# Seven edits to the order of work in a fused attention and mixture-of-depths kernel

## The chip, the cores and the metric

The kernel runs on one core of a Trainium2 chip. The metric is the device time of one execution in microseconds (us), of which several runs are taken. A core has five engines that run side by side and wait for one another by semaphores: TensorE (PE, matrix products and transposes; its weight loads are listed as PEld), VectorE (DVE), ScalarE (ACT), GpSimd (POOL) and SyncE (SP), which here only issues transfers (DMAs). Each engine takes its instructions in the order in which the program emits them.

## The reference, cut to what matters

```python
# attention, per batch (8) and head (12), sequence 448, head size 64
q_n = q / sqrt(mean(q*q) + 1e-6) * g_q          # k_n likewise, with g_k
attn = softmax(q_n @ k_n.T / sqrt(64))
x = concatenate heads of (attn @ v)             # [8, 448, 768]
# mixture of depths, per batch
scores = x @ w_gate                             # [448]
top = the 128 tokens with the highest scores
h = maximum(x[top] @ w1, 0)                     # w1 [768, 1024]
out = x;  out[top] = x[top] + sigmoid(scores[top])[:, None] * (h @ w2)   # w2 [1024, 768]
```

All is float32.

## The kernel before, in words

**Groups and units.** The attention is cut into 24 groups (`q`, or `n`, from 0 to 23), three for each batch, of four heads each. A group has seven units of 64 keys. For a unit, `scores` (L337) multiplies keys by queries into two PSUM banks of the pool `ps_sc` (four banks), and two exponentials on ACT (L346) write a probability tile `p` (seven buffers, two heads side by side). The key's norm is applied as the scale of the exponential. `values` (L361) multiplies the values by `p`. `add_probs` adds the probability tiles of a group on DVE (L377), so that `sum_keys` (L404) can get the denominators by small products on PE with `pick_pair`. `by_array(n)` says for how many of a group's last units that addition is left out: these tiles are kept in `lasts` and given to PE as further terms of the same sum. After that, `invert_sums` transposes and inverts the denominators (`rden`, L420) and `to_tokens` transposes the result to tokens and scales it (L435, L437) into the batch's tile `x`.

**Norms.** Queries and keys come in twice, transposed for the products (`qT`, `kT`) and by tokens (`tok`). `squares` (L255, ACT) squares a `tok` tile into one of two buffers `sqs`, `sum_squares` (L264, DVE) sums it and POOL raises the sum to the power -1/2 (L265). For queries this goes out to DRAM (`rows_out`, L276), comes back spread over the partitions (`rows_in`, `bc`, L287), and `scale_q` (L296, DVE) multiplies `qT` by it before the group's scores. `prepare` (L773) sets the times of all this for a group.

**The mixture.** For each batch, `gate` (L463, DVE) takes the products of `x` and the gate's weights after every group, 256 columns at a time; `spread` sums the three parts. `ranks_of` transposes the gate's scores so that every token sees all (L488 on PE, L494 on ACT), `count` (L504, DVE) counts the higher ones, `annotate` writes gate and token number into two more columns of `x`, and `select` scatters the chosen rows to DRAM by four indirect DMAs from POOL (L531). `load_selected` (L549) reads them back by SP into `xe`, which has three buffers. `mixture(g)` then works on two batches at once, as a block product with seven products instead of eight in each of the two layers (a scheme of Strassen's kind): weights are kept as three blocks and four differences (numbers 0 to 3). In the first mixture the differences are made on DVE (`mix`, L244), stored to DRAM (`mixed`, L224) and later read back (`load_mixed`, L221) into a ring of three buffers; `used` asks for the next one when one is done. Products go to a PSUM bank `main`, or to a `side` bank that is taken from `ps_sc`. `share` copies or adds a product into the hidden layer (L658 on ACT, L660 on DVE), and the relu of a sum is L662 on ACT. `gated` (L578, DVE) applies the gate to the second layer's products, and `write` (L569) scatters the rows to the output from POOL.

**Order.** The schedule is written out by hand. The emission order is the order of each engine's queue. `at(slot, fn)` puts a call in a list under a unit's number, and `run(upto)` calls all that are due. Groups 0 to 7 have two places for that, after units 3 and 6. From group 8 on (`FIRST`) all seven units of a group come first (a stretch), and then three gaps: denominators of the group before, `run(u0 + 1)` and a piece of the mixture; `invert_sums`, the first `to_tokens`, `run(u0 + 3)` and a piece; the second `to_tokens`, `run(u0 + 6)` and in some groups a piece. `soon()` gives the present slot. After the last group the remaining pieces run one after another: this is the tail.

Of the kernel before, what the change touches and what calls it, by code (L numbers as in the profile page):

```python
# [68 lines left out]
def fast(  # L69
# [156 lines left out]
    def mix(l, i, part):  # L226

        if part == 0:
            if i == 3:
                in_ring(l, 3)  # L230
            elif i == 1:
                ring[l, 1] = ring[l, "B12"]
            elif i == 2:
                in_ring(l, 2)
            else:
                ring[l, 0] = ring[l, 2]
        a, b = {
            3: (blocks[l, (1, 1)], ring[l, "B12"]),
            1: (ring[l, "B12"], blocks[l, (0, 0)]),
            2: (blocks[l, (1, 1)], ring.get((l, 1))),  # L240
            0: (blocks[l, (1, 0)], ring.get((l, 2))),
        }[i]
        f = chunk(part)
        nc.vector.tensor_tensor(out=ring[l, i][:, f], in0=a[:, f], in1=b[:, f], op=OP.subtract)  # L244
# [145 lines left out]
    def by_array(n):  # L390

        return 2 if n < 2 * NG else 1 if n == n_groups - 1 else 0
# [62 lines left out]
    def gate(n):  # L455

        b, g = divmod(n, NG)
        if g == 0:
            gates[b] = moe_pool.tile([CP, NJ, NG], F32, name="gate_parts", bufs=2)
        cols = slice(GH * D * g, GH * D * (g + 1))  # L460
        for j in range(NJ):
            prod = moe_pool.tile([CP, S], F32, tag="wide", name="prod")
            nc.vector.scalar_tensor_tensor(  # L463
                out=prod[:, 0 : GH * D],
                in0=xs[b][:, j, cols],
                scalar=1.0,
                in1=wg[:, cols],
                op0=OP.mult,
                op1=OP.mult,
                accum_out=gates[b][:, j, g : g + 1],  # L470
            )
# [75 lines left out]
    def load_selected(b):  # L547
        xe = moe_pool.tile([128, DX], F32, name="xe", bufs=3)
        nc.sync.dma_start(out=xe[:CAP], in_=slots_dram.pop(b))  # L549
        xes[b] = xe  # L550
# [4 lines left out]
    def mixture(g):  # L555
# [41 lines left out]
        def used(l, i):  # L597

            if not to_load or g == 0 and (l == 1 or i == 2):
                return  # L600
            what = to_load.pop(0)
            s = soon()
            for part in range(2):
                at(s + 4 + 2 * part if s >= 0 else s, load_mixed, *what, part)
# [47 lines left out]
        def share(k, ps, begun):  # L652
            h = {1: h11, 2: h12, 3: h21, 4: h22}[k]
            ps = ps.rearrange(flat, t=128)[:, :, :n]
            missing[k] -= 1
            last_one = missing[k] == 0
            if not begun:
                nc.scalar.activation(out=h[:, :, :n], in_=ps, func=AF.Relu if last_one else AF.Copy)  # L658
                return
            nc.vector.tensor_tensor(out=h[:, :, :n], in0=h[:, :, :n], in1=ps, op=OP.add)  # L660
            if last_one:
                nc.scalar.activation(out=h[:, :, :n], in_=h[:, :, :n], func=AF.Relu)  # L662

        begun = set()
# [9 lines left out]
        for k in (1, 2, 3, 6, 5, 7, 4) if g == 0 else (1, 2, 6, 5, 7, 3, 4):  # L674
            in_main, what, a, targets = todo_products[k]
            ps = main if in_main else side()
            product(ps, weights(1, what), a(), k == 1 or not in_main)
            for t in targets:
                share(t, ps, t in begun)
                begun.add(t)  # L680
# [8 lines left out]
            if g == 0:  # L689
                if k == 5:  # L690
                    mix_all(1, 0)
                if k == 7:
                    for part in range(2):
                        load_block(2, (0, 1), part)
            yield
# [27 lines left out]
        for k in (1, 2, 6, 5, 7, 3, 4):  # L723
# [24 lines left out]
            if g == 0:  # L748
                if k == 1:
                    mix_all(2, 3)  # L750
                    mix_all(2, 1)
                if k == 2:
                    mix_all(2, 2)
                if k == 5:
# [18 lines left out]
    def prepare(n, slot):  # L773
        sq = {}
        for i in range(2):
            at(slot + 2 * i, lambda i=i: sq.setdefault(i, squares(n, i)))
            at(slot + 2 * i + 1, lambda i=i: sum_squares(n, i, sq.pop(i)))

        at(slot + (7 if n > 2 else 6), rows_out, n)
        at(slot + (10 if n > 5 else 9 if n > 2 else 8), rows_in, n)  # L780

    for n in range(1, n_groups):
# [4 lines left out]
        if n > 1:  # L787
# [3 lines left out]
            first = max(s0 - (20 if n > 5 else 17), 0)  # L791
            prepare(n, first)
            at(max(s0 - 6, first + 11), scale_q, n)
# [3 lines left out]
    for k, i in enumerate((3, 1, 2)):  # L797
        for part in range(2):
            at(NI * FIRST + 2 * k + part, mix, 1, i, part)
            at(NI * FIRST + 2 * k + part + 3, store_mixed, 1, i, part)  # L800
# [3 lines left out]
    def after_tokens(n):  # L804
        b, g = divmod(n, NG)
        s = soon()
        at(s + (2 if n == 1 else 0), gate, n)
# [3 lines left out]
        at(s + 4 if s >= 0 else s, store_x, b)  # L811
        at(s + 1 if s >= 0 else s, spread, b)

    def ranks_of(b):
# [6 lines left out]
        at(s + 7 if s >= 0 else s, load_selected, b)  # L821
# [28 lines left out]

    def run(upto):
# [13 lines left out]
    for q in range(n_groups):  # L865
# [4 lines left out]
        if q < FIRST:  # L870
            for place, us in enumerate(((0, 1, 2, 3), (4, 5, 6))):
                for i in us[::2]:
# [3 lines left out]
                    run_values(u0 + i - 1 if i < NI - 1 else u0 + i - 2, hold=i == us[2])  # L876
                slot[0] = u0 + us[0]
# [20 lines left out]
        for i in range(0, NI, 2):  # L898
# [3 lines left out]
            run_values(u0 + i - 1 if i < NI - 1 else u0 + i - 2)  # L902
        slot[0] = u0
# [3 lines left out]
        if g == 1 and b > 2:  # L907
# [3 lines left out]
        slot[0] = u0 + 2  # L911
        invert_sums(q - 1)
# [561 lines left out]
```

## Time and profile before

| | us |
|---|---|
| median of 3 runs (546.56 to 550.29) | 548.3 |
| the profiled execution | 549.26 |
| its span, first to last instruction | 547.5 |
| PE busy | 492.2 |
| DVE busy | 381.1 |
| ACT busy | 284.5 |
| POOL busy | 189.7 |

All times in the text are from the start of the span. In lists of groups, a line names the code line, the engine, the operation, what it writes and reads, how often, the busy time in all and the mean of one in ns. In lists of waits, a line says who waited for whom, the total, how often, and the longest. In the timeline a line has start, length, engine, code line, operation and tiles; `[5.79 <-DVE hT L660]` is the idle time of that engine before it and what ended it. Stages: start-up until 11.5, groups 0 to 7 until some 141, groups 8 to 23 with mixtures 0 to 2 until some 458, then the tail with the rest of mixture 2, the last batch's ranks and mixture 3.

### The profile page before, as it was taken

How to read it: one execution, taken by the hardware profiler on the slowest of the kernel's cores; microseconds unless marked ns; L12 is line 12 of the kernel's file. 1: busy time of each engine (PE TensorE's matmuls, PEld its weight loads, DVE VectorE, ACT ScalarE, POOL GpSimd, SP SyncE). 2: the span in 40 equal slices, each digit the busy share in tenths (PEclk: the TensorE clock that was granted, in tenths of full speed). 3: DMA queues.
4: the chain of work that ended last, by engine and by line, in shares of the span. 5: the costliest groups of instructions: out<-in, count | busy, mean ns of one | idle time of the engine just before them, and what ended most of it. 6: DMA issues, size and time to landing. Idle time of an engine off the chain costs nothing. (4 is left out here: it accounts for less than half of the span.)

```text
span 547.5 us, 11644 instructions
## 1 busy us (share of the span) xinstructions
PE 492.2 (90%) x4605; PEld 295.7 (54%) x4605; DVE 381.1 (70%) x718; ACT 284.5 (52%) x519; POOL 189.7 (35%) x104
## 2 busy tenths in 40 slices
PE   5979999989959889799979999999979999939990
PEld 4534444434726574364556785554455657628860
DVE  4653779799984767899878687887977784812240
ACT  4875788767626457365656647538565662002100
POOL 4682355744350307123452307321660030110002
PEclk9998999999979899999999999999999999978997
DMA  8877889799693473877778683979392351445711
GB/s 313 328 227 261 260 256 303 237 312 302 225 282 117 155 265 95 291 251 276 265 249 266 204 274 109 295 239 342 98 277 84 104 172 60 167 146 192 228 63 62
DMA packets 54449, 118.43 MB, mean 216 GB/s; under 512 B 12115, under 2 KB 26452, under 8 KB 54386
## 3 DMA queue, kind: packets, MB, share of 16 engines
q1 hardware_dynamic: 50978, 111.28, 63.1%
q0 software_dynamic: 3264, 6.31, 3.5%
q8 instruction: 38, 0.62, 0.5%
q14 instruction: 25, 0.20, 0.1%
q10 hardware_dynamic: 144, 0.00, 0.0%
HBM read 93.81 MB, written 31.64 MB: 229 GB/s over the span
## 5 line engine op out<-in xcount | busy, mean ns | idle before, releaser
L346 ACT ACTIVATE p<-sc,rinv 128x448 f32<-128x448 f32 x336 | 188.3, 640 | 92.7 <-issue 48.3
L265 POOL TENSOR_TENSOR rinv<-ss,neg_half 128x14 f32<-128x14 f32 (+1 forms) x49 | 134.2, 2742 | 196.4 <-DVE ss L264 146.6
L337 PE MATMUL sc<-qT,kT 64*64 64x448 f32 x1344 | 171.9, 553 | 14.5 <-DVE hT L660 5.8
L361 PE MATMUL av<-p,v 64*64 64x448 f32 x1344 | 165.5, 548 | 0.4 <-ACT xT L384 0.3
L377 DVE TENSOR_TENSOR sum<-sum,p 128x896 f32<-128x896 f32 x107 | 116.8, 1091 | 16.3 <-ACT p L346 11.0
L337 PEld LDWEIGHTS sc<-qT,kT 64*64 64x64 f32 x1344 | 61.8, 134 | 85.3 <-issue 43.7
L361 PEld LDWEIGHTS av<-p,v 64*64 64x64 f32 x1344 | 68.2, 136 | 65.9 <-issue 54.5
L531 POOL DMA_INDIRECT selected<-x,rank x32 | 39.7, 1240 | 68.6 <-DVE x L523 60.4
L264 DVE TENSOR_REDUCE ss<-sq 128x14 f32<-128x910 f32 (+1 forms) x49 | 52.3, 1072 | 0.7 <-ACT sq L255 0.7
L437 DVE TENSOR_TENSOR x<-x_ps,rden 112x512 f32<-112x512 f32 x48 | 32.8, 688 | 22.5 <-PE x_ps L435 20.6
L255 ACT ACTIVATE sq<-tok 128x896 f32<-128x896 f32 (+1 forms) x49 | 44.3, 936 | 7.3 <-DMA tok<-in_tok_dram 3.2
L463 DVE SCALAR_TENSOR_TENSOR prod<-x,wg 112x256 f32<-112x256 f32 x96 | 40.6, 423 | 2.6
L569 POOL DMA_INDIRECT out_dram<-xe,row x10 | 9.8, 984 | 85.8 <-DVE xe L578 37.9
L435 PE MATMUL x_ps<-ident,xT 128*112 128x128 f32 x192 | 29.1, 275 | 5.1 <-DVE rden L420 5.1
L578 DVE SCALAR_TENSOR_TENSOR xe<-moe_ps,xe 128x384 f32<-128x384 f32 (+2 forms) x17 | 10.0, 590 | 32.9 <-PE moe_ps L705 32.9
L662 ACT ACTIVATE hT<-hT 128x512 f32<-128x512 f32 x12 | 7.6, 630 | 46.5 <-DVE hT L660 46.5
L504 DVE SCALAR_TENSOR_TENSOR cmp<-score_rows,gate,earlier 112x448 f32<-112x448 f32 x32 | 21.8, 683 | 13.2 <-ACT score_rows L494 12.5
L384 ACT COPY xT<-av 128x448 f32<-128x448 f32 x48 | 23.4, 539 | 10.1 <-PE av L361 6.9
L377 DVE TENSOR_TENSOR sum<-p 128x896 f32<-128x896 f32 x24 | 26.1, 1086 | 2.1 <-ACT p L346 2.1
L435 PEld LDWEIGHTS x_ps<-ident,xT 128*112 128x112 f32 x192 | 21.6, 133 | 10.3 <-DVE rden L420 6.9
L296 DVE SCALAR_TENSOR_TENSOR qT<-qT,gg,bc 128x896 f32<-128x896 f32 x22 | 25.2, 1145 | 0.0
L643 PE MATMUL moe_ps<-xeT,ring 128*128 128x128 f32 x192 | 23.1, 277 | 1.8 <-DVE hT L660 1.8
(83 smaller groups left out, 459.1 us busy)
## 6 DMA issues: line engine op xcount, KB each, us to landing
tok<-in_tok_dram SPq DMA_DIRECT2D x48, 448.0 KB
ring<-mixed SPq DMA_DIRECT2D x48, 384.0 KB
qT<-in_qT_dram SPq DMA_DIRECT2D x24, 448.0 KB
kT<-in_kT_dram SPq DMA_DIRECT2D x24, 448.0 KB
v<-in_vp_dram SPq DMA_DIRECT2D x24, 448.0 KB
out_dram<-x SPq DMA_DIRECT2D x8, 1344.0 KB
bc<-rows SPq DMA_DIRECT2D x44, 224.0 KB
mixed<-ring SPq DMA_DIRECT2D x16, 384.0 KB
```

Source lines behind the costliest of these rows:

```text
L255: nc.scalar.activation(out=sq[:, h, :, 0:D], in_=t[:, h], func=AF.Square, scale=scale)
L264: nc.vector.tensor_reduce(out=ss[:, h], in_=sq[:, h], axis=AX.X, op=OP.add)
L265: nc.gpsimd.tensor_tensor(out=rinv[:, h].rearrange(flat), in0=ss[:, h].rearrange(flat), in1=neg_half.to_broadcast([128, (h.stop - h.start) ...
L296: nc.vector.scalar_tensor_tensor(out=t, in0=t, scalar=gg, in1=bcs.pop(n), op0=OP.mult, op1=OP.mult)
L337: nc.tensor.matmul(out=scs[hh][D * c : D * (c + 1), 0:S], lhsT=get("kT", n)[r, c, D * i : D * (i + 1)], rhs=get("qT", n)[r, c, :], start=True,
L346: nc.scalar.activation(out=p[:, hh], in_=scs[hh][:, 0:S], func=AF.Exp, scale=rinvs[n, 1][:, hh, i : i + 1],)
L361: nc.tensor.matmul(out=avs[n][c][D * hh : D * (hh + 1), 0:S], lhsT=get("v", n)[r, hh, i, :], rhs=probs[u][r, hh], start=(i == 0), stop=(i ...
L377: nc.vector.tensor_tensor(out=sums[n], in0=probs.pop(u - 1) if begins else sums[n], in1=probs.pop(u), op=OP.add)
L435: nc.tensor.transpose(out=ps[:CP, j, :], in_=t[:, j, :], identity=ident)
L437: nc.vector.tensor_tensor(out=xs[b][:, :, col : col + 128].rearrange("p j (h d) -> p j h d", d=D), in0=ps[:CP].rearrange("p j (h d) -> p j ...
L463: nc.vector.scalar_tensor_tensor(out=prod[:, 0 : GH * D], in0=xs[b][:, j, cols], scalar=1.0, in1=wg[:, cols], op0=OP.mult, op1=OP.mult, ac ...
L531: w = nc.gpsimd.indirect_dma_start(out=t[:, :], out_offset=bass.IndirectOffsetOnAxis(ap=rank[:, j : j + 1], axis=0), in_=x[:, j, :], in_of ...
```

## The change

Seven edits, all to the order, the place or the split of work:

1. *Squares.* `prepare` spreads the two squares and two sums of a group over four places, one each; rows go out and come back at new times.
2. *Queries.* `scale_q` is no longer in the list of due calls. A new `scale_queries(upto)` calls it, in groups 0 to 7 right after the units of a place and ahead of everything else there, later at the head of the second gap.
3. *Relu.* `share` no longer issues the relu of a sum; it is issued after the matmuls of the next product, and at once after the last product.
4. *Gate.* Nothing after the first group of a batch, 448 columns after the second, 320 after the third.
5. *Differences.* T3 is made from T2 less a kept block, not from the block B12, and later: in the first layer after the other two, in the second after product 6. The reads of the ring follow (`used`).
6. *Ranks.* In groups 13 and 19 (g = 1, b even) `ranks_of(b - 1)` comes after the first four units of the stretch and all its counting is issued there; the load of the rows comes a slot earlier for batches above 1.
7. *Last rows.* The last batch's rows are loaded into a `p` tile, and by POOL's queue instead of SP's.

`by_array` also gives 2 for all groups below 14 instead of below 6, and `store_x` comes one slot earlier.

```diff
         a, b = {
-            3: (blocks[l, (1, 1)], ring[l, "B12"]),
+            3: (ring.get((l, 2)), blocks[l, (0, 0)]),
...
-        return 2 if n < 2 * NG else 1 if n == n_groups - 1 else 0
+        return 2 if n < 14 else 1 if n == n_groups - 1 else 0
...
         if g == 0:
-            gates[b] = moe_pool.tile([CP, NJ, NG], F32, name="gate_parts", bufs=2)
-        cols = slice(GH * D * g, GH * D * (g + 1))
+            return
+        if g == 1:
+            gates[b] = moe_pool.tile([CP, NJ, 2], F32, name="gate_parts", bufs=2)
+        cols = slice(0, S) if g == 1 else slice(S, DM)
...
-        xe = moe_pool.tile([128, DX], F32, name="xe", bufs=3)
-        nc.sync.dma_start(out=xe[:CAP], in_=slots_dram.pop(b))
+        if b < B - 1:
+            xe = moe_pool.tile([128, DX], F32, name="xe", bufs=3)
+        else:
+            xe = p_pool.tile([128, 2, S], F32, name="p").rearrange("p h s -> p (h s)")[:, 0:DX]
+        queue = nc.gpsimd if b == B - 1 else nc.sync
+        queue.dma_start(out=xe[:CAP], in_=slots_dram.pop(b))
...
-            if not to_load or g == 0 and (l == 1 or i == 2):
+            if not to_load or g == 0 and (l == 1 or i in (2, 3)):
                 return
-            what = to_load.pop(0)
             s = soon()
-            for part in range(2):
-                at(s + 4 + 2 * part if s >= 0 else s, load_mixed, *what, part)
+            for _ in range(2 if g == i == 0 else 1):
+                what = to_load.pop(0)
+                for part in range(2):
+                    at(s + 4 + 2 * part if s >= 0 else s, load_mixed, *what, part)
...
             if last_one:
+                summed.append(h)
+
+        def relu_summed():
+            while summed:
+                h = summed.pop(0)
                 nc.scalar.activation(out=h[:, :, :n], in_=h[:, :, :n], func=AF.Relu)
...
             product(ps, weights(1, what), a(), k == 1 or not in_main)
+            relu_summed()
...
+            if k == 4:
+                relu_summed()
             yield
...
                 if k == 1:
-                    mix_all(2, 3)
                     mix_all(2, 1)
                 if k == 2:
                     mix_all(2, 2)
+                if k == 6:
+                    mix_all(2, 3)
...
-    def prepare(n, slot):
+    urgent = {}
+
+    def prepare(n):
         sq = {}
+        s2, s1 = NI * (n - 2), NI * (n - 1)
+        late_rows, late_scale = n - 2 >= FIRST, n - 1 >= FIRST
+        times = [s2 - 2, s2, s2 + 2, s2 + 5] if n > 2 else [0, 0, 5, 7]
         for i in range(2):
-            at(slot + 2 * i, lambda i=i: sq.setdefault(i, squares(n, i)))
-            at(slot + 2 * i + 1, lambda i=i: sum_squares(n, i, sq.pop(i)))
-
-        at(slot + (7 if n > 2 else 6), rows_out, n)
-        at(slot + (10 if n > 5 else 9 if n > 2 else 8), rows_in, n)
+            at(times[2 * i], lambda i=i: sq.setdefault(i, squares(n, i)))
+            at(times[2 * i + 1], lambda i=i: sum_squares(n, i, sq.pop(i)))
+        at(3 if n == 2 else s2 + 3 if late_rows else s2 + 4, rows_out, n)
+        at(5 if n == 2 else s2 + 5 if late_rows else s1, rows_in, n)
+        urgent[s1 + (2 if late_scale else 4)] = n
...
-            first = max(s0 - (20 if n > 5 else 17), 0)
-            prepare(n, first)
-            at(max(s0 - 6, first + 11), scale_q, n)
+            prepare(n)
...
-    for k, i in enumerate((3, 1, 2)):
-        for part in range(2):
-            at(NI * FIRST + 2 * k + part, mix, 1, i, part)
-            at(NI * FIRST + 2 * k + part + 3, store_mixed, 1, i, part)
+    for k, (i, part) in enumerate([(1, 0), (1, 1), (2, 0), (2, 1), (3, 0), (3, 1)]):
+        first = NI * FIRST + k + (3 if i == 3 else 0)
+        at(first, mix, 1, i, part)
+        at(first + 3, store_mixed, 1, i, part)
...
-        at(s + 7 if s >= 0 else s, load_selected, b)
+        at(s + (6 if b > 1 else 7) if s >= 0 else s, load_selected, b)
...
+    def scale_queries(upto):
+        for x in [x for x in urgent if x <= upto]:
+            scale_q(urgent.pop(x))
+
...
+                scale_queries(u0 + us[-1])
                 slot[0] = u0 + us[0]
...
+            if i == 2 and g == 1 and b % 2 == 0:
+                slot[0] = u0 - 2
+                ranks_of(b - 1)
+                run(u0)
         slot[0] = u0
         sum_keys(q - 1)
         if q == FIRST:
             to_tokens(q - 2, 1, ps_sc)
-        if g == 1 and b > 2:
+        if g == 1 and b % 2 == 1:
             ranks_of(b - 1)
         run(u0 + 1)
         next(moe)
         slot[0] = u0 + 2
+        scale_queries(u0 + 3)
         invert_sums(q - 1)
```

## The prediction

> **What bounds the kernel now.** I read the page's summary, then the waits of TensorE (PE), then the timeline around each of its long waits, then the queues of the engines that ended them.
>
> ```profile
> span 547.5 us, 11644 instructions
> ...
> PE 492.2 (90%) x4605; PEld 295.7 (54%) x4605; DVE 381.1 (70%) x718; ACT 284.5 (52%) x519; POOL 189.7 (35%) x104
> ...
> PE   5979999989959889799979999999979999939990
> ```
>
> PE has work for 492 of 547.5 us. The rest is start-up (4.9), a tail of 11.6 after the last matmul (535.9 to 547.5), and some 39 us of gaps. No engine but PE is near full overall; gaps are what a change can win. The waits of PE:
>
> ```profile
> PE moe_ps L705 <- DMA ring<-mixed: 8.4, 1, 8.4
> PE xeT_ps L611 <- DMA xe<-selected: 6.5, 3, 3.2
> PE sc L337 <- DVE hT L660: 5.8, 1, 5.8
> PE x_ps L435 <- DVE rden L420: 5.1, 4, 3.1
> ...
> PE sc L337 <- issue: 3.2, 2, 2.9
> PE sc L337 <- DVE x L437: 1.8, 1, 1.8
> PE moe_ps L643 <- DVE hT L660: 1.8, 1, 1.8
> PE sc L337 <- ACT hT L658: 1.6, 1, 1.6
> ```
>
> Two kinds: transfers that come late (the first two rows), and VectorE (DVE) or ScalarE (ACT) that is behind. The largest, in the tail, as the timeline has it:
>
> ```profile
> 484.17 0.98 POOL L569 DMA_INDIRECT out_dram<-xe,row  x1 [3.26 <-DVE xe L578]
> 487.37 0.32 SPq L549 DMA_DIRECT2D xe<-selected  x1
> 487.81 37.33 SPq L221 DMA_DIRECT2D ring<-mixed  x18
> ...
> 491.62 4.87 PE L705 MATMUL moe_ps<-ring,hT 128*128 128x384 f32 x8 [8.38 <-DMA ring<-mixed]
> ```
>
> The last batch's rows need one of three `xe` buffers, so their load on SP's queue waits for the write of batch 4's rows at 484.17; the weight block for PE's next product is queued behind it. Its eight matmuls then take 4.87 us where the eight before took 2.74: the granted clock is 0.61 in 483.3 to 496.3. The next largest:
>
> ```profile
> 158.54 0.68 DVE L660 TENSOR_TENSOR hT<-hT,side_ps 128x512 f32<-128x512 f32 x1
> 159.13 0.55 DVE L588 TENSOR_TENSOR xeT<-xeT,hT 128x384 f32<-128x384 f32 x1
> 159.25 0.63 ACT L662 ACTIVATE hT<-hT 128x512 f32<-128x512 f32 x1 [10.81 <-DVE hT L660]
> 159.27 0.19 PEld L337 LDWEIGHTS sc<-qT,kT 64*64 64x64 f32 x3 [6.56 <-DVE hT L660]
> 159.27 1.01 PE L337 MATMUL sc<-qT,kT 64*64 64x448 f32 x3 [5.79 <-DVE hT L660]
> ```
>
> DVE comes late to one addition; ACT stands 10.81 us before the relu of it with exponentials queued behind, and PE waits for the side product's PSUM bank, which that addition frees.
>
> [...]clock 0.91, 0.88, 0.93 and 0.61 in the stretches with gaps of 2.89, 5.79, 1.65 and 8.38, but 1.00 after three gaps near 3.1. [...]no plain load on POOL is in this trace. [...]
>
> **The change part by part**, against the profiled execution's 549.26 us (span 547.5 and 1.8 around it; the median of the runs is 548.3, 1 lower).
>
> *Last rows into a probability tile, from POOL.* The last of four scatters starts at 479.96; the median to landing is 3.1, so the load can go at 483.1. On SP such a load took 3.9 (issue 397.84, reader 401.73 in the other late case); I take 3.9 for POOL[...]. Rows at 487.0. The weight block is no longer behind it: its buffer is free when the product of 472.75 ends (475.5), so it lands before 483.24. PE does that product by 486.0, six transposes by 486.9, the others at once. The first product of the last mixture then starts near 488.2 instead of 497.64: **-9.4**. The write at 484.17 now queues behind the load on POOL; nobody needs it. The wider last gate (below) adds 0.35 on the path (row transposes wait for it at 469.73): **-9.1**.
>
> *Den sums by PE for n below 14 instead of 6.* Eight groups (6 to 13) lose two additions each on DVE: 16 x 1.09 = 17.4 us, mostly in 130 to 270, where DVE is busy 17 to 19 of 20. PE gets two terms more a group: the 208 instructions of 13 terms are 6.3 us, 0.485 each, so 16 terms are **+7.7**, on the bound engine, all counted. Two `p` tiles are held longer, but the first later addition frees two at once, so ring pressure is about as before: 0 (bounds -1, +3).
>
> *Gate in two parts.* 12 x (0.423+0.081) a batch becomes 4 x (0.683+0.082) for 448 columns (the row of `cmp`, same size and form) and 4 x (0.51+0.08) for 320, interpolated: 6.05 to 5.43, -5 us on DVE in all. But it moves: none for the first group of a batch (-2.0), +1.0 for the second, +0.35 for the third. Where DVE ended a PE wait that is +1.0 (gap of 1.84 at 115.3, second group).
>
> *The 5.79 gap, relu a product later, T3 from T2.* DVE is busy without a break from 143.5 to 159.2. Ahead of the addition go: two sums (-2.2), the first group's gate (-2.0), two mixes that now come a stretch later (-1.9); the second group's gate adds 1.0. Sum -5.1, so a wait of 0.6 is left. Relu no longer blocks the exponentials. The slow matmuls after it come back too (a mean clock of 0.88 over the 29 us from 152 is 7.0 at half rate; some 5 of them fall on work after 159.27, half of that lost, 2.5): -5.2 - 2.5 = -7.7, and -0.7 for the `rden` wait at 148.5: **-8.4**. At 183, the relu no longer holds ACT's read of the side bank, but DVE's addition does (gate +0.35): 1.65 to about 0.75, and half of a slow window (1.7): **-1.8**. At 200.8 the reduce moves ahead of the counts into 3 us in which DVE waits: **-1.1**. At 224.5, two of four mixes go (-1.8) but the query scaling comes ahead of `rden` (+1.15): **-0.5**.
>
> *Ranks in mid-stretch.* For batches 3 and 5 the counts move half a stretch (some 8 us) earlier and the load one gap earlier, against waits of 3.06 and 3.20: **-6.2**. It puts the row transposes into a score bank and two ACT operations (0.53+0.21) between exponentials, twice: **+1.0** (0 to 3). SP waits at that load, queued ahead of later loads; those are needed a stretch later.
>
> *Squares one gap apart, queries first.* Early on DVE waits 4.63 us for the denominators with the scaling of group 2 behind them (39.92); PE idles 2.89 and runs half rate (2.95 for 16 matmuls that take 1.73 elsewhere; 1.7 in all). Scaled first, it fits into that idle time: **-4.6**. The squares that hold ACT at 67.55 no longer wait for a reduce: **-1.2**. The 0.93 wait for a sum at 123.5 goes with its additions: -0.9. With the gate's +1.0: **-5.7** early. Later the scaling stands before `rden` in the second gap. A 2.75 us product hides it mostly; at 347.06 the margin is 0.2 us and at 421.77 there is a wait already, so **+2.0** (0 to 6).
>
> Sum: -9.1 +7.7 -8.4 -1.8 -1.1 -0.5 -6.2 +1.0 -5.7 +2.0 = -22.1, so 527.2 against the profiled time, 526.2 against the median. I forecast **527**.
>
> **The rivals.**
> *PE pays, DVE stays late* (0.11). Only the transfers come earlier (-15.3), and the rest is given back by whatever DVE does next: -15.3 + 7.7 + 3 = -4.6, so 545. For: DVE at 19 of 20 in places. Against: 17.4 + 5 us leave it.
> *All gaps go* (0.13). Gaps of 0.25 us and more after start-up add to 36.7, their slow clock to 8.0: -44.7 + 7.7, 512. Against: PE waits at 115 and 224 have causes that stay.
> *Slower: scaling waits for its rows* (0.06). For groups 3 to 9 the rows go out and come back later than before, and the scaling heads an in-order DVE. From sum to scaling there are about 1.5 groups, 21 us; the chain is 1.1 + 2.7 + rows (9.4 seen, 31.89 to 41.29) + broadcast (4 to 9): 17 to 22. From about 21 on it bites; 4 us late in 7 groups is +28, with the early gain gone: 549.3 - 22.1 + 5.7 + 28, 561. Against: SP waits less, since rows out and in no longer stand side by side, and 4.4 and 3.9 were usual later.
> *The POOL load is slow*, so the tail isn't what it says: at 7 us it costs 3, 530, inside the main case.
>
> **How the numbers follow.** The main case has 0.70 and spans 517 to 537 (unknown costs: scaling -2/+4, ranks -1/+2, POOL -1/+3, `p` tiles -1/+3, clock windows and DVE's lag 5 either way). A measurement here tells no change from 1%, 5.5 us. Faster by more: 0.70 + 0.13 + 0.03 of the first rival, 0.86; within: 0.08; slower: 0.06. The range of 8 in 10 reaches from the all-gaps case to just short of the first rival: 512 to 541.
>
> **What would show it.** No PE wait for `ring<-mixed` in the tail and no clock below 0.9 there; `xe<-selected` gone from PE's waits; `den_ps<-p` at 464 instructions near 14 us; DVE busy near 359 us; ACT's waits for `hT` L660 (46.5 us) mostly gone; no 0.88 stretch near 159. Wrong if DVE shows waits before the scaling of `qT`, if `rden` ends more PE waits than now, or if the `p` exponentials wait for sums.

## The result and the profile after

The changed kernel takes **544.6 us** (median of 20 runs, 539.08 to 547.34), the kernel before 549.0 on the same chips (545.46 to 551.99): a ratio of **0.992**, 95% interval [0.989, 0.995], some 4 us less. The forecast was 527, its range 512 to 541: right in sign, wrong in size. Ratios leave out executions more than 1.5% above the fastest of their kernel; medians keep them. The profiled execution took 540.99 us, one of the faster ones. The head of its page, to be read against the lines of before:

```profile
span 539.3 us, 12042 instructions
...
PE 490.4 (91%) x4861; PEld 294.5 (55%) x4861; DVE 361.3 (67%) x638; ACT 284.2 (53%) x519; POOL 188.1 (35%) x105
...
PE   5999897978999899899999999999998999969990
```

DVE lost 20 us of work (381.1 to 361.3), as forecast (359), and PE's busy time fell by 2, but the row of PE still has weak slices: in the first third, and near the end. The waits of PE after:

```profile
PE sc L335 <- issue: 11.1, 4, 3.3
PE x_ps L433 <- DVE rden L418: 6.5, 6, 2.5
PE xeT_ps L617 <- DMA p<-selected: 5.3, 1, 5.3
...
PE sc L335 <- ACT hT L664: 1.4, 1, 1.4
PE moe_ps L649 <- DVE hT L666: 0.9, 1, 0.9
...
PE sc L335 <- DVE hT L666: 0.5, 1, 0.5
```

The waits of 8.4 for `ring<-mixed`, 6.5 for `xe<-selected` and 5.8 for `hT` are gone (0.5 is left of the last). Two new ones stand in their place: 11.1 us in four places, put down to "issue" because the profile names no releaser, and 5.3 us in the tail for the last batch's rows. The starts of groups divide the span into three stages (us, profiled executions):

| stage | before | after | difference | forecast |
|---|---|---|---|---|
| start to group 8 | 130.44 | 134.29 | **+3.9** | -5.7 |
| group 8 to the end of the scores | 321.24 | 309.75 | **-11.5** | -7.3 |
| tail | 95.79 | 95.24 | **-0.5** | -9.1 |

(-7.3 is the forecast's sum without its early and its tail step; some 1.0 of the extra terms in it, those of group 6, falls into the early stage.) The middle won more than forecast. Some 9.5 us are missing in the early stage and 8.6 in the tail.

**Early.** The timeline of VectorE after, in group 3, where group 4's queries are scaled at L294:

```profile
60.62 1.08 DVE L375 TENSOR_TENSOR sum<-p 128x896 f32<-128x896 f32 x1
61.62 1.09 DVE L262 TENSOR_REDUCE ss<-sq 128x14 f32<-128x910 f32 x1
62.63 0.61 DVE L463 SCALAR_TENSOR_TENSOR prod<-x,wg 112x448 f32<-112x448 f32 x1
...
65.17 2.28 DVE L375 TENSOR_TENSOR sum<-sum,p 128x896 f32<-128x896 f32 x2
67.37 1.15 DVE L294 SCALAR_TENSOR_TENSOR qT<-qT,gg,bc 128x896 f32<-128x896 f32 x1
```

TensorE in the same stretch, at the first scores of group 4:

```profile
68.62 3.07 PE L335 MATMUL sc<-qT,kT 64*64 64x448 f32 x16 [3.29 <-issue]
```

And VectorE in the same part of the kernel before:

```profile
66.37 1.09 DVE L264 TENSOR_REDUCE ss<-sq 128x14 f32<-128x910 f32 x1
67.38 1.14 DVE L296 SCALAR_TENSOR_TENSOR qT<-qT,gg,bc 128x896 f32<-128x896 f32 x1
...
69.45 0.41 DVE L463 SCALAR_TENSOR_TENSOR prod<-x,wg 112x256 f32<-112x256 f32 x1
...
71.19 2.22 DVE L377 TENSOR_TENSOR sum<-sum,p 128x896 f32<-128x896 f32 x2
```

Before, the scaling stood ahead of the gate and ahead of the next two sums. Now it stands behind both: the group's first scores wait 3.29 us and start 0.1 us after the scaling ends. It was due at `max(s0 - 6, first + 11)`, one unit into the group before, and so taken in that group's *first* place. It is now due at `s1 + 4`, and the first place only takes what is due up to `s1 + 3`: "ahead of everything else" holds for the *second* place, where the queue already holds the first place's gate and the sums of units 2 and 3 (the x2 at 65.17). Group 2 was always in the second place, and gained (it starts at 37.65 instead of 41.17).

**Tail.** What answers to the three lines of the forecast, in the timeline after:

```profile
472.67 0.94 POOL L531 DMA_INDIRECT selected<-x,rank  x1 [0.30 <-issue]
...
479.03 0.60 POOL L554 DMA_DIRECT2D p<-selected  x1 [5.42 <-PE xeT_ps L617]
...
484.46 1.54 PE L617 MATMUL xeT_ps<-ident,p 128*128 128x128 f32 x6 [5.27 <-DMA p<-selected]
...
485.80 4.24 PE L649 MATMUL moe_ps<-xeT,w 128*128 128x128 f32 x24
```

And in SP's own queue:

```profile
468.25 30.65 SPq L221 DMA_DIRECT2D ring<-mixed  x12
```

The load from POOL goes out 6.4 us after the start of the fourth scatter (3.1 was forecast), and PE can use the rows 5.4 us later. (The profile puts POOL's wait down to PE's transposes of other rows, which the load doesn't need; the fourth scatter landed at 478.06, just ahead.) Meanwhile SP, which no longer stands at the load of the rows, moves weight blocks from 468.25 on; before, this block of SP's work only began at 487.81. From 481.89 to 488.72, in and after the wait, PE runs at half clock (0.50 granted): the product of 24 matmuls takes 4.24 us, the next like it 2.84.

Part of the loss lies at the very end. The rows that the last mixture writes go out from POOL, one write after another. The second of these writes:

```profile
528.86 0.96 POOL L574 DMA_INDIRECT out_dram<-p,row  x1 [4.95 <-DMA out_dram<-xe,row]
```

The same write in the first of the tail experiments below, where SP loads the last rows:

```profile
522.78 0.96 POOL L573 DMA_INDIRECT out_dram<-p,row  x1 [2.85 <-DMA out_dram<-xe,row]
```

From the last matmul to the end of the span the changed kernel takes 14.2 us, the kernel before 12.0. So of the 8.6 us some 4.9 are the late start of the last mixture's first product, 1.4 its slow clock, and 2.2 stand here.

### The profile page after: what moved, and what is told of

It reads as the page before. It is cut to its first block, busy times and chain, and to the rows that moved or that the text cites. A ratio compares the mean times of both kernels' runs of the same rounds, so it can differ in the third digit from the quotient of the medians.

```text
span 539.3 us, 12042 instructions
## 1 busy us (share of the span) xinstructions
PE 490.4 (91%) x4861; PEld 294.5 (55%) x4861; DVE 361.3 (67%) x638; ACT 284.2 (53%) x519; POOL 188.1 (35%) x105
## 5 line engine op out<-in xcount | busy, mean ns | idle before, releaser
L335 PE MATMUL sc<-qT,kT 64*64 64x448 f32 x1344 | 163.4, 552 | 15.7 <-issue 11.1
L359 PE MATMUL av<-p,v 64*64 64x448 f32 x1344 | 155.7, 542 | 0.0
L375 DVE TENSOR_TENSOR sum<-sum,p 128x896 f32<-128x896 f32 x91 | 99.2, 1090 | 17.5 <-ACT p L344 13.5
L335 PEld LDWEIGHTS sc<-qT,kT 64*64 64x64 f32 x1344 | 57.7, 134 | 84.4 <-issue 55.4
L359 PEld LDWEIGHTS av<-p,v 64*64 64x64 f32 x1344 | 62.7, 134 | 66.9 <-issue 60.4
L531 POOL DMA_INDIRECT selected<-x,rank x32 | 36.8, 1151 | 62.6 <-DVE x L523 54.8
L463 DVE SCALAR_TENSOR_TENSOR prod<-x,wg 112x448 f32<-112x448 f32 (+1 forms) x64 | 35.7, 558 | 2.1
L294 DVE SCALAR_TENSOR_TENSOR qT<-qT,gg,bc 128x896 f32<-128x896 f32 x22 | 25.2, 1145 | 6.0 <-DMA bc<-rows 4.7
L574 POOL DMA_INDIRECT out_dram<-xe,row x7 | 7.7, 1105 | 50.1 <-DVE xe L583 35.9
L583 DVE SCALAR_TENSOR_TENSOR xe<-moe_ps,xe 128x384 f32<-128x384 f32 x14 | 8.6, 614 | 22.2 <-PE moe_ps L719 22.2
L649 PE MATMUL side_ps<-xeT,w 128*128 128x128 f32 x192 | 23.1, 277 | 0.0
```

Source lines behind the costliest of these rows:

```text
L335: nc.tensor.matmul(out=scs[hh][D * c : D * (c + 1), 0:S], lhsT=get("kT", n)[r, c, D * i : D * (i + 1)], rhs=get("qT", n)[r, c, :], start=True,
L359: nc.tensor.matmul(out=avs[n][c][D * hh : D * (hh + 1), 0:S], lhsT=get("v", n)[r, hh, i, :], rhs=probs[u][r, hh], start=(i == 0), stop=(i ...
L375: nc.vector.tensor_tensor(out=sums[n], in0=probs.pop(u - 1) if begins else sums[n], in1=probs.pop(u), op=OP.add)
L463: nc.vector.scalar_tensor_tensor(out=prod[:, 0 : cols.stop - cols.start], in0=xs[b][:, j, cols], scalar=1.0, in1=wg[:, cols], op0=OP.mult, ...
L531: w = nc.gpsimd.indirect_dma_start(out=t[:, :], out_offset=bass.IndirectOffsetOnAxis(ap=rank[:, j : j + 1], axis=0), in_=x[:, j, :], in_of ...
L649: nc.tensor.matmul(out=ps[:, 128 * f : 128 * f + n], lhsT=w[:, d, 128 * f : 128 * (f + 1)], rhs=h[:, d, :n], start=first and f == d == 0, ...
```

## The experiments

All edits are made to the changed kernel. Ratios are to the kernel before, which ran beside each of them (its medians are 548.3 to 552.4 us, so the ratios are compared and not the times); the changed kernel has 0.9916, and 0.01 is 5.5 us. Starts of groups and lengths of stretches are those of one profiled execution.

### The early scaling back in the first place

```diff
-        urgent[s1 + (2 if late_scale else 4)] = n
+        if n == 2 or late_scale:
+            urgent[s1 + (2 if late_scale else 4)] = n
+        else:
+            at(s1 + 1, scale_q, n)
```

It then stands behind the gate, but ahead of the two sums.

> The changed kernel, with the query scaling of groups 3 to 8 put back into the first place of the group before, behind the gate but ahead of the last two sums (the rows still come back when the changed kernel asks for them). Theory 1 (the scaling stands too far back in DVE's queue: gate, wider by 1.0 us, and two sums of 1.1 us now go ahead of it): the four PE waits of 3.29, 2.82, 2.85 and 2.16 us before groups 4, 5, 7 and 8 go, with the slow matmuls after the first (1.7 us), so 8 to 11 us less than the changed kernel, group 8 starting near 125 us instead of 134.3. Rival 1 (the spread rows land late, so DVE waits for them wherever the scaling stands): DVE shows waits for bc before qT of several us, and the gain is under 3 us.

Measured: 537.8 us, ratio 0.975 [0.969, 0.982], 8.9 us below the changed kernel. Its timeline of VectorE before group 4:

```profile
64.64 1.15 DVE L294 SCALAR_TENSOR_TENSOR qT<-qT,gg,bc 128x896 f32<-128x896 f32 x1
65.70 2.29 DVE L375 TENSOR_TENSOR sum<-sum,p 128x896 f32<-128x896 f32 x2
```

Its waits of PE for scores:

```profile
PE sc L335 <- DVE x L435: 2.0, 1, 2.0
PE sc L335 <- issue: 1.7, 1, 1.7
...
PE sc L335 <- ACT sq L253: 1.1, 1, 1.1
```

The 11.1 us in four places are down to 1.7 in one, with 1.09 of the old wait at group 4 now under another name; the wait of 2.0, in group 7, is new. Group 8 starts at 128.39 instead of 134.29; 125 was expected. The place in the queue was the cause of the four waits. The rival, that the rows of the norms come too late, does not explain them: in the changed kernel DVE waits twice for rows, 1.81 us at 277.74 and 2.92 at 395.46, never ahead of these four scalings, and no wait of PE follows from the two.

With the scaling further forward, though, the rows are the next limit. Here DVE waits 0.96 us for them at 108.42, and PE's remaining 1.7 us stand right behind that scaling. The kernels below that keep this repair have such waits too. The longest, ahead of group 6, in one execution of the kernel with both repairs and without the extra terms:

```profile
96.01 1.15 DVE L294 SCALAR_TENSOR_TENSOR qT<-qT,gg,bc 128x896 f32<-128x896 f32 x1 [5.04 <-DMA bc<-rows]
...
97.27 3.13 PE L335 MATMUL sc<-qT,kT 64*64 64x448 f32 x16 [3.67 <-issue]
```

### The last rows by SP, behind one weight block

```diff
-        queue = nc.gpsimd if b == B - 1 else nc.sync
-        queue.dma_start(out=xe[:CAP], in_=slots_dram.pop(b))
+        nc.sync.dma_start(out=xe[:CAP], in_=slots_dram.pop(b))
...
-    for _ in moe:
+    for k, _ in enumerate(moe):
         run(units)
+        if k == 1:
+            load_selected(B - 1)
```

The last batch's load in `ranks_of` is dropped with it. The `p` tile as the destination stays.

> The changed kernel, with the last batch's rows still read into a probability tile, but by SP, queued right behind the weight block for the product before and ahead of the other four weight loads. Theory 2 (freed from waiting, SP now sends four weight loads of 384 KB through the DMA engines while the last scatter and the rows' load are under way; these take 5.4 and 5.4 us where 3.1 and 3.9 were usual): the rows land 4 to 5 us earlier, the PE wait of 5.27 us before the last mixture's transposes shrinks to about 1, no half clock after it, 5 to 6 us less than the changed kernel. Rival 2 (the scatter itself is slow or PE's wait has another cause): the wait stays above 4 us.

Measured: 541.1 us, ratio 0.979 [0.971, 0.987], 6.8 us below the changed kernel; in the profile the tail is 84.9 us instead of 95.2. Its timeline there:

```profile
476.64 0.94 POOL L531 DMA_INDIRECT selected<-x,rank  x1 [0.30 <-issue]
...
479.52 0.32 SPq L553 DMA_DIRECT2D p<-selected  x1
...
482.98 0.82 PE L616 MATMUL xeT_ps<-ident,p 128*128 128x128 f32 x6
...
483.64 2.84 PE L648 MATMUL moe_ps<-xeT,w 128*128 128x128 f32 x24
```

The load goes out 2.9 us after the scatter's issue, PE doesn't wait for the rows, and the product takes 2.84 us. This is what the forecast's tail step had described, and within this stage it is worth what that step said (-9.1 forecast, -10.9 against the kernel before). The 10.3 us between the two tails are the wait of 5.3, 2.1 of slow clock behind it, and 2.8 after the last matmul. The whole profile is only 6.4 us shorter, since its earlier stages took 4.0 longer, with code that is the same there.

### The same, behind three weight blocks

The last edit with `k == 3` in place of `k == 1`: six transfers of SP, as in the changed kernel, move beside the scatters, but the load is SP's.

> As the tail's repair (the last rows by SP), but the load stands behind three weight blocks of SP (six transfers), not behind one: SP's blocks then move while the four scatters do, as in the changed kernel; only the queue of the load differs from it. Theory (the competing transfers hold the last scatter back, whatever the queue): the last scatter takes about 5 us again, the load goes out near the fifth us after it and TensorE waits 4 to 6 us for p<-selected, with the tail near 95 us and a ratio of about 0.99. Rival (the load is slow because POOL issues it): the last scatter takes 3 us, the rows land some 3 us later, TensorE waits less than 1.5 us and the tail is near 86 us, ratio 0.98.

Measured: 541.3 us, ratio 0.984 [0.978, 0.991], which overlaps with the changed kernel's; the tail is 89.5 us. The load goes out at 481.26, 5.0 us after the scatter of 476.26. PE in the timeline:

```profile
485.41 0.87 PE L616 MATMUL xeT_ps<-ident,p 128*128 128x128 f32 x6 [2.64 <-DMA p<-selected]
486.12 4.47 PE L648 MATMUL moe_ps<-xeT,w 128*128 128x128 f32 x24
```

| tail | SP's transfers beside the scatters | scatter to load, us | load to PE's use, us | PE waits, us |
|---|---|---|---|---|
| changed kernel | 6, and 2 just ahead of the load | 6.4 | 5.4 | 5.27 |
| rows by SP, behind one block | 2 | 2.9 | at most 3.5 | none |
| rows by SP, behind three | 6 | 5.0 | 4.2 | 2.64 |

Both expectations missed the size. With six of SP's transfers beside it the fourth scatter took 4.56 us with the load in SP's queue and 5.03 with the load in POOL's (those of the kernel before landed within 2.8 to 3.6), and half of the wait is there. The single DMA packets in the two traces show where the other half went:

| us | fourth scatter's start to its last packet | to the load's issue | to the load's first packet | to PE's use |
|---|---|---|---|---|
| changed kernel | 5.03 | 1.33 | 2.89 | 2.54 |
| rows by SP, behind three | 4.56 | 0.44 | 1.42 | 2.73 |

Of the 2.6 us between them 0.9 lie before the issue and 1.5 between issue and first packet. In the six kernels here that load these rows from POOL the two steps take 1.3 to 1.4 us and 2.0 to 2.9, in the six that load them into the `p` tile from SP 0.4 and 0.9 to 1.4. So the change of queue carries at least the 0.9; in the 1.5 the fourth block may have a part, whose two transfers SP issues within 0.5 us ahead of POOL's load. The end of the tail goes with the queue as well: from the last matmul to the end of the span the six kernels with POOL's load take 14.0 to 14.3 us, all others 11.4 to 12.0. Why a plain load from POOL should slow a later write from POOL stays open.

### The last rows as before

Buffer `xe` again, and the load by SP in its old place: edit 7 undone.

> The changed kernel with the last rows again in an xe buffer and loaded by SP as in the kernel before. The prediction's step said that this edit is worth 9.1 us. Theory 2 (half of it is lost to the competing loads): 3 to 5 us slower than the changed kernel, with the PE wait of about 8.4 us for the weight block back. Rival (the edit is worth what was forecast, and something else in the tail ate it): 8 to 10 us slower.

Measured: 550.0 us, ratio 0.999 [0.994, 1.003]; the tail is 95.6 us. In PE's waits:

```profile
PE moe_ps L714 <- DMA ring<-mixed: 8.4, 1, 8.4
```

The old wait is back in full, yet the tail is only 0.3 us longer than in the changed kernel: edit 7 exchanged one wait for another, and for a later end. The 3.9 us between the ratios aren't in the tail; this profile has 17 us at half clock in and just behind the early stage, where the code is the same (see the last section).

### The denominators' extra terms

`by_array` gives 2 for n below 6 again.

> The changed kernel with by_array giving 2 only below group 6 as before. The prediction counted all of the 7.7 us of extra PE work as cost, and let DVE's relief (17.4 us) pay only through single waits. By that sum, taking it back gives PE 7.7 us less work, and waits for DVE of about 4 us come back: 3 to 4 us faster than the changed kernel. Rival (in groups 8 to 14 DVE is as full as PE, and its lateness costs more than the extra work): slower by 2 to 8 us, with PE waits for hT L666, rden or sum back in 140 to 260 us.

Measured: 546.2 us, ratio 0.989 [0.982, 0.996], not separable from the changed kernel. From group 8 to group 14 it takes 127.4 us against 131.1, but with one half-clock stretch in it against two. A cleaner pair stands further below.

### The relu at once

```diff
-                summed.append(h)
+                nc.scalar.activation(out=h[:, :, :n], in_=h[:, :, :n], func=AF.Relu)
```

> The changed kernel with the relu of a sum issued right behind the sum, as before. Theory: the relu's own share of the forecast 8.4 + 1.8 us is small, since PE waits for the side bank that DVE's addition frees, and DVE is no longer late there: 1 to 3 us slower than the changed kernel, ACT's waits for hT back at 30 us or more. Rival: the exponentials queued behind the relu were the true cause of the 5.79 us wait and its slow clock: 6 us or more slower, with that wait back near 155 us.

Measured: 548.6 us, ratio 0.996 [0.993, 0.999], 2.5 us above the changed kernel, with intervals that overlap a little. The timeline where the 5.79 us gap was:

```profile
163.66 0.68 DVE L666 TENSOR_TENSOR hT<-hT,side_ps 128x512 f32<-128x512 f32 x1
...
164.38 0.63 ACT L668 ACTIVATE hT<-hT 128x512 f32<-128x512 f32 x1 [7.78 <-DVE hT L666]
...
164.40 1.02 PE L335 MATMUL sc<-qT,kT 64*64 64x448 f32 x3 [3.97 <-DVE hT L666]
```

And in the changed kernel:

```profile
160.73 0.60 PE L335 MATMUL sc<-qT,kT 64*64 64x448 f32 x3 [0.51 <-DVE hT L666]
```

With the relu in its old place a wait of 3.97 us is there again, though DVE has all its relief. DVE is no later than in the changed kernel: in both, the addition ends 5.6 us after group 9's first scores (7.4 before). What differs is that ACT stands 7.78 us with the exponentials behind the relu, and PE, which in the changed kernel goes on to its next scores meanwhile, stands too. Group 9 takes 27.70 us; it takes 23.10 in the changed kernel and took 29.70 before. So, slow clock included, the later relu carries 4.6 us of the 6.6 there and DVE's lighter queue 2.0, which lies between the two expectations. My working had put the gap to DVE's lateness and let the relu free ACT on top.

### The ranks in the gap

`ranks_of` in the gap for all batches above 1, and the load at its old slot: edit 6 undone.

> The changed kernel with the ranks of batches 3 and 5 in the first gap again and the loads of the rows a slot later, as before. Forecast step: 6.2 us less waiting for 1.0 us of disturbance, so 5 us slower than the changed kernel, with two PE waits of about 3 us for xe<-selected back near 280 and 398 us. Rival: hidden by something else, under 2 us.

Measured: 546.3 us, ratio 0.989 [0.983, 0.994], no slower than the changed kernel. In PE's waits:

```profile
PE xeT_ps L617 <- DMA xe<-selected: 0.5, 1, 0.5
```

The two waits of 3 us do not return. Groups 14 and 20 take 20.42 and 16.82 us against 19.77 and 16.33 in the changed kernel and 22.26 and 19.72 before: the ranks' move is worth 1.1 us, and other parts of the change the other 4.7. Which parts was not isolated. Before, the first scatter of batch 3 stood on POOL behind a power at 270.93, which fits the new times of the squares.

### Both repairs

The early scaling and the rows by SP, together.

> The two repairs together: query scaling of groups 3 to 8 ahead of the last sums of its place, and the last rows read by SP right behind the one weight block. If the two losses are separate, their gains add: 8.9 + 6.8 us less than the changed kernel by the two runs before, so a ratio to the kernel before of 0.963 or so. If they are not, no better than 0.975.

Measured: 521.9 us, ratio **0.952** [0.948, 0.955]. Twenty-two us below the changed kernel, more than the two gains added (15.7). The granted clock by slices, of the changed kernel:

```profile
PEclk9999989999999899899999999999999999988995
```

And of this one:

```profile
PEclk9999999999999999999999999999999999999996
```

No slice but the last is slow in this execution. The surplus of 6.3 us is not shown to be one: the intervals of the four ratios together leave some 6 us open. The mean granted clock is on record for every execution: 0.981 to 0.991 in the six of this kernel, of which the profiled one is the best, and 0.963 to 0.978 in the twenty of the changed kernel. So this kernel loses less to the clock in all of its executions, and in the profiled one it was also lucky: gaps of 2.48 and 2.03 us are left in it and drew no half clock (see the last section).

### Both repairs, without the extra terms

The last kernel with `by_array` giving 2 for n below 6. It ran twice, the second time beside the kernel below.

> The two repairs, and by_array again 2 only below group 6. In the profile without the new by_array the stretch from group 8 to group 14 took 127.4 us against 131.1 to 131.6 with it, though the runs could not tell the two. If the extra PE work of 7.7 us costs about 4 us net, this is 3 to 4 us faster than the two repairs alone. If the relief of DVE pays for it, the same or slower.

> The kernel with both repairs and the old number of denominators by TensorE again, only to stand beside the next one on the same chip: 0.947 of the kernel before, waits for rden of 6 to 7 us.

Measured: 520.4 and 519.8 us, ratios 0.947 [0.943, 0.951] and 0.947 [0.943, 0.950]. That is some 2.5 us better than with the terms, in two sets of runs whose intervals overlap with it a little. From group 8 to 14 it takes 124.3 us in both profiles, with the terms 127.9, and none of the three has half clock there: 3.6 us. On this path the terms cost more than DVE's relief brings.

### The later scaling ahead of the piece

```diff
         run(u0 + 1)
+        scale_queries(u0 + 3)
         next(moe)
         slot[0] = u0 + 2
-        scale_queries(u0 + 3)
         invert_sums(q - 1)
```

First on the changed kernel, then on the one with both repairs and without the terms.

> The changed kernel, but from group 8 on the scaling of the next group's queries stands at the head of the piece of the mixture in the first gap, not behind it ahead of the inversion. Theory (the scaling of 1.15 us delays rden, as the step of +2.0 says): the waits of TensorE for rden, 6.5 us in 6, fall to about 3.5, and the time is 1.5 to 3 us below the changed kernel's (0.986 to 0.989 of the kernel before, where the changed one has 0.992). Rival (the waits for rden come from the mixes and the gate, the scaling hides anyway): rden waits stay at 6 and the ratio at 0.992; it can be above that if the scaling now delays the additions of the piece behind it.

> Both repairs, the old number of denominators by TensorE, and the later scaling at the head of the first gap's piece. Theory: waits for rden fall from 7.0 us to about 3.5, so 1.5 to 3 us below the kernel beside it (0.942 to 0.944 of the kernel before). Rival: no difference, 0.947.

Measured: 540.7 us, ratio 0.985 [0.981, 0.990], 3.4 us below the changed kernel, with intervals that touch; and **516.8 us**, ratio **0.942** [0.939, 0.945], 3.0 below the kernel beside it, again with a small overlap. PE's waits in the first:

```profile
PE x_ps L433 <- DVE rden L418: 3.0, 4, 1.4
...
PE moe_ps L649 <- DVE hT L666: 2.0, 1, 2.0
```

And in the second:

```profile
PE x_ps L433 <- DVE rden L418: 4.1, 4, 1.4
PE xeT_ps L616 <- DMA xe<-selected: 3.1, 1, 3.1
```

The waits for `rden` fall from 6.5 and 7.0 to 3.0 and 4.1; one wait for an addition, 0.9 us in both kernels beside, becomes 2.0, and in the second kernel a wait for rows has grown from 0.8 to 3.1, which leaves something to win. The waits fall as the theory said, and the times lie where it put them. The last kernel is the fastest of all, 5.8% below the kernel before.

## Why the prediction was wrong, step by step

**Early, -5.7 forecast, +3.9 measured: the step that failed first.** "Scaled first, it fits into that idle time" was worked out at group 2 alone, where it held (groups 1 and 2 took 4.2 us less, 4.6 forecast), and carried to the other groups by the words "scaled first". For them the change moved the scaling later, from the first place of a group to the second, behind a gate that had become wider (+1.0 was counted, at one wait only) and two sums of 1.1 us each. With the scaling back in the first place and the old denominators, three profiles with the same code in this stage have group 8 start at 130.45, 127.17 and 125.16: 0 to -5.3 against before. So most of what was forecast is there to be won in the best of them, and the edit didn't win it; in the others late rows and half clock take it back.

**Tail, -9.1 forecast, -0.5 measured: the second.** "The median to landing is 3.1, so the load can go at 483.1" took the scatter's time from a stretch in which SP stood still. The same sentence's change set SP free. I had noted that the weight block is no longer behind the load, and not that the weight blocks would then move beside the scatters. The load went out 3.3 us later after the scatter's start than forecast, and the rows took 1.5 more: the 3.9 was the time of SP's load, not shown for POOL, where it took 5.4. The time of the scatter had no bounds. The end of the tail, 2.2 us longer, was put at nothing.

**Middle, -7.3 forecast, -11.5 measured.** The wait near 159 went as said (0.51 left, 0.6 forecast), its cause more to the relu than I had it. At 183 only 0.2 us of the wait went, not 0.9, and a stretch at half clock stayed (3.4 us from 181.52). The ranks' -6.2 were right in their sum (groups 14 and 20 lost 5.9 us) and wrong in their cause: 1.1 were theirs. The extra terms are 464 instructions of 13.9 us, as said, but the +7.7 was mis-sized as a cost: from group 8 to 14, where some 5.8 of it falls, they cost 3.6, so DVE's relief pays the rest back. These 2.2, and the 1.0 that falls into the early stage, are most of the 4.2 us that the middle won beyond the forecast; the rest was not isolated. The later scaling (+2.0) was worth 3.0 to 3.4, inside its bounds of 0 to 6.

**The rivals.** *PE pays, DVE stays late* has the measured time, 545, but not its mechanism: DVE did not stay late in the middle, and in the tail the transfers did not come earlier. *Scaling waits for its rows* named the right instruction at the head of DVE's queue, but the cause was its place there, not the rows; these bite only where the scaling is further forward (0.96 us in the first experiment). That an edit might do another thing than its words say was not among my rivals, and it was what decided: with the early scaling and the rows put where the forecast had assumed them, the same change takes 521.9 us.

**The signs.** The waits for `ring<-mixed` and `xe<-selected` are gone, there is no slow stretch near 159, DVE's busy time came as named, and ACT's waits for the addition ahead of a relu fell from 46.5 to 13.3 us. The clock in the tail did not stay above 0.9: it is at half for 6.8 us from 481.89. Of the signs of being wrong two appeared. DVE waits before the scaling of `qT` (4.7 us, none before), which cost nothing here, and `rden` ends six waits of PE, 6.5 us, instead of four of 5.1, which is the later scaling's +2.0. Neither is the step that failed.

## What to carry to other kernels

Where work is placed by due times, work out for every group in which place an edited due time is taken, and list what is then ahead of it in that engine's queue; one group that gains says nothing of the others. Here a DMA queue that waited also held traffic back (freed, SP moved its weight blocks from 468.25 on, not from 487.81, and scatter to load took 6.4 us; it took 2.9 with two of SP's transfers beside it and the load by SP): whoever frees such a queue must time the transfers on the path again, with that traffic beside them. Put the load that the path waits for ahead of the loads that can wait, in the queue that issues it first; here that was SP's, 0.4 us after the scatter's last packet, where POOL's took 1.3 to 1.4.

## What the runs showed of the hardware

**The same gap can cost nothing or some 1.5 us.** The four early gaps of 2.2 to 3.3 us are in every kernel with the scaling in the second place. The granted clock (third figure from the end of each row) in the windows behind them, in the changed kernel with the later scaling moved:

```profile
67.30:74.10 6.80, 5.44 (x32) 2.17 (x36) 4.13 (x6) 2.31 (x4) 2.42 (x1) 0.50 0.61 210
87.70:91.10 3.40, 3.09 (x20) 1.23 (x24) 3.26 (x7) 1.16 (x2) 0.00 (x0) 0.51 1.06 405
121.90:125.30 3.40, 3.40 (x21) 1.52 (x24) 3.29 (x11) 2.04 (x4) 0.00 (x0) 0.50 0.42 130
138.90:142.30 3.40, 3.40 (x24) 1.46 (x20) 2.39 (x3) 2.12 (x4) 2.79 (x3) 0.51 0.70 242
```

And in the changed kernel itself:

```profile
67.30:74.10 6.80, 5.48 (x41) 2.56 (x45) 4.08 (x6) 2.79 (x6) 2.47 (x1) 0.75 0.59 190
86.90:90.30 3.40, 3.31 (x36) 1.69 (x40) 3.26 (x8) 2.18 (x4) 0.00 (x0) 1.00 1.02 379
117.90:121.30 3.40, 3.34 (x30) 1.53 (x34) 3.26 (x8) 1.92 (x4) 0.00 (x0) 1.00 1.04 384
134.20:137.60 3.40, 3.31 (x36) 1.69 (x40) 2.86 (x4) 2.17 (x4) 2.79 (x3) 1.00 1.04 398
```

Seventeen us at half rate in the one, 3.4 in the other, with nearly the same gaps. Group 5, which begins with one of these windows, takes 15.74 us in the one and 14.20 in the other.

What goes with it can be read from the traces. All half-clock stretches of an execution, up to the last matmul, begin on one grid of 3.413 us and last one to three of its steps: in the changed kernel they begin at 68.88, 181.52, 222.48 and 481.89, which are 33, 12 and 76 steps apart. Whether the clock falls goes, in these traces, with how long PE was busy in the step just before. PE's busy time, of 3.41 us, in the steps over which the four gaps lie:

| gap before group | changed kernel | with the later scaling moved |
|---|---|---|
| 4 | 0.26, then half clock | 1.53, then half clock |
| 5 | 1.64 and 2.37, full clock | 0.86, then half clock |
| 7 | 1.86 and 2.12, full clock | 1.37, then half clock |
| 8 | 1.81 and 2.85, full clock | 1.25, then half clock |

So here it mattered how much of a gap fell into one step: the gap of 3.29 us before group 4 left 0.26 us of work in its step and was followed by half clock, while those before groups 5, 7 and 8, split over two steps, left 1.64 us or more in each and were not. After the start-up, in the fourteen traces together, 53 steps at full clock were followed by half clock, all with less than 2.0 us of work, and none with less than 1.4 was followed by full clock; between these bounds both occur. The kernels before and after have eight of the 53, with 0.00 to 1.97 us of work; the least work that full clock followed is 1.53 us there. In the changed kernel half clock followed a gap as short as 1.44 us (it ends at 181.3), with 1.97 us of work in its step. The grid does not lie alike in all executions: counted back from the half-clock stretches, its first step begins 0.6 us after the start of the span in the changed kernel and, as an estimate from the windows above, 2.4 us after it with the later scaling moved. So which gaps cost is partly luck. The changed kernel's times go with the granted clock: the nine of its executions with a mean clock of 0.963 took 545.5 to 547.3 us, the two with 0.978 took 539.1 and 539.2. One profiled execution is a poor witness for a few us.
